# A tenth pair of chunks shares its weights in an attention and MoE kernel: the first chunk's transposed weights serve the fifth

## The chip, the cores and the metric

The kernel runs on one core of one Trainium2 chip. The metric is device time in microseconds (us): the median of three runs for the kernel before, and a profiled execution beside them that all rows below come from.

## What is computed

Two stages, cut from the reference to what matters here (8 batches, 2496 tokens, model width 256, key width 64, 8 experts of width 1024):

```python
scores = (1.0 / S) * np.matmul(z, z.transpose(0, 2, 1))
attn = np.maximum(scores, 0.0) ** 2
out = u * np.matmul(attn, v)
# then, on the rows of out with x @ w_skip > 0: top-1 expert, x + gate * (relu(x @ w1[e]) @ w2[e])
```

The scores of one batch are z times its own transpose, so the matrix of weights is symmetric: the weights of keys in group j for queries in chunk c are the transpose of those of keys in group c for queries in chunk j. The kernel uses this.

## The kernel before, in words

**Chunks and steps.** The queries of each batch are cut into five chunks of 512 tokens (the fifth has 448). I call them first to fifth; the code has c = 0 to 4. A chunk works through ten steps p = 0 to 9, each of 256 keys, so that steps 2j and 2j+1 are the keys of chunk j. `ORDER[c]` is the table that sets in which order a chunk takes its steps; batch 0's first chunk takes them 0 to 9. I call the position in that order the *place*, 0 to 9.

**One step.** `weights` (L322 to L338) makes the weights of a step: either it computes scores on TensorE (`scores`, L276, three pairs of half-row matmuls into `ps`) and ScalarE makes relu and square of them (L324, L325) in a tile `r`; or it takes `r` from memory (`recall`, L309 for a full chunk, L311 and L312 for the fifth). Then the high part `ah` is cast (L334, on ScalarE or VectorE as `on_act` says: on ScalarE for every step that belongs to a pair or stands in `EXTRA[c]`), and VectorE makes the low part `al` (L338). `attend` (L365) multiplies both with the values: up to 24 half-row matmuls for the two halves d = 0 and 1 of the width, and 18 for step 9, whose last keys are half a block.

**Pairs.** `PAIRS` lists the pairs (c, j) of chunks that share weights. For a pair, chunk c computes the steps of group j and `keep` (L293) turns them on VectorE, two transposes a step, into a tile `rt`; there are two such tiles for the whole kernel, and one pair fills one. When both steps are in, four stores (L720, 256 KB each) put the tile in a memory tensor `kept`. Chunk j later loads the two steps with `recall` and computes no scores for them. Batch 0 uses no pair with the first chunk.

**The order of the work.** The program is written out by hand, engine by engine, and each queue runs in order; SyncE (SP) issues the loads and stores. At each place the loop issues a recall five places ahead (`ahead`), makes weights two places ahead (`stage`), attends d = 0 of the step at hand and then d = 1. Place 8 attends only d = 0; place 9 ends the chunk, and its d = 1 work covers both. `keep` of the step at place 8 is put off by a place. What ends a chunk runs in the next one: row transposes of the output (L402) after places 1 and 2, stores `xr` and `out` (L411, four each) after places 3 and 4, and the stores of `kept` by `put_some` two places after their tile was filled. In every other first chunk (batches 1, 3, 5, 7) the routing of two chunks' tokens also runs, a run of small VectorE operations (L514 to L530 among them).

```python
t = turned_r[ci] = gp.tile([P, QC // 32, P], F32, name="rt", tag="rt", bufs=2)   # in keep, for even p
r = ap.tile([P, 2, QC], F32, name="r", tag="r", bufs=5)                          # in r_tile
after = [(rows0, 2), (rows1, 3), (store, 4), (store, 5)]                         # places after a chunk's end
```

Before the first load lands, TensorE runs `NWARM` small matmuls (L177). After the 40 chunks come the expert layers (L632, L651), which the change does not touch.

Of the kernel before, what the change touches and what calls it, by code (L numbers as in the profile page):

```python
# [22 lines left out]
NSTAT = 8  # L23
NFIX = 3
NARM = 2 * (NSTAT - NFIX)
NWARM = 35

PAIRS = ((0, 1), (0, 2), (0, 3), (1, 2), (1, 3), (1, 4), (2, 3), (2, 4), (3, 4))  # L30
ORDER = (
# [5 lines left out]
)  # L37
EXTRA = ((8,), (3,), (4, 5), (6, 7), (0, 1, 8))

# [9 lines left out]
def attn_moe(ctx, tc, zT, uT, v, wg, w1, w2, cst, pad, out):  # L49
# [125 lines left out]
    psw = ps_s.tile([P, 2, QC], F32, name="psw", tag="s")  # L175
    for _ in range(NWARM):
        nc.tensor.matmul(psw[:32, 0, :64], ones[:, :32], ones[:, :64], start=True, stop=True)  # L177
# [49 lines left out]
    def pairs(b):  # L227

        return PAIRS if b else [x for x in PAIRS if x[0]]

# [10 lines left out]

    kept = {x: dram.tile([QC, QC], F32, name="kept%d%d" % x) for x in PAIRS}
    HALF = (slice(0, 64), slice(64, 128))
# [804 lines left out]
```

## Time and profile before

| | us |
|---|---|
| median of three runs (lowest, highest) | 1758.07 (1756.36, 1759.94) |
| the profiled execution | 1756.26 |
| its span, first to last instruction | 1754.5 |
| TensorE busy (PE) | 1741.5 (99%) |
| VectorE busy (DVE) | 1176.2 (67%) |
| ScalarE busy (ACT) | 1154.4 (66%) |
| GpSimd busy (POOL) | 511.8 (29%) |
| DMA, mean over the span | 160 GB/s |

The attention part fills the first 1262 us or so of the span, the expert layers the rest. A chunk takes 27 to 35 us. In the rows, PE is TensorE, DVE VectorE, ACT ScalarE, SP SyncE; SPq is the issue of a transfer by SP. "out<-in" are tile names, and "[0.51 <-PE ps L276]" is idle time of the engine before the row and what ended it. Start times count from the start of the span.

### The profile page before, as it was taken

What the parts mean: (1) busy time and instruction counts of PE and PEld (TensorE: products, weight loads), DVE (VectorE), ACT (ScalarE), POOL (GpSimd) and SP (SyncE); (2) the same over time, 40 slices, a digit from 0 to 9 for tenths busy, and PEclk for the clock granted to TensorE, in tenths of its full rate; (3) what the DMA queues carried; (4) which work ended last, traced back from release to release, by engine and by line L of the source; (5) the groups of instructions that cost most, each with busy time, mean ns of one, the idle gap of its engine ahead of it and who ended that gap; (6) DMA issues with size and microseconds to landing.
All of it is one profiled execution on the core that took longest, in us unless ns stands there. A gap on an engine that the chain in (4) does not pass through costs nothing.

```text
span 1754.5 us, 39820 instructions
## 1 busy us (share of the span) xinstructions
PE 1741.5 (99%) x15783; PEld 1554.9 (89%) x15783; DVE 1176.2 (67%) x1912; ACT 1154.4 (66%) x1435; POOL 511.8 (29%) x516
## 2 busy tenths in 40 slices
PE   9999999999999999999999999999999999999998
PEld 7888888988888898888889888888999999999998
DVE  6877877787787788778778877777753433343333
ACT  8877877887787778778787887877533333333321
POOL 1102202212311221231222032122356456635731
PEclk9999999999999999999999999999999999999999
DMA  5667689387768848875784888477553323313210
GB/s 193 151 173 178 165 219 263 90 224 227 195 146 214 227 129 205 255 206 126 214 231 125 201 243 230 113 207 207 160 133 89 80 80 112 95 51 93 88 39 27
DMA packets 432353, 281.00 MB, mean 160 GB/s; under 512 B 213844, under 2 KB 370902, under 8 KB 432033
## 3 DMA queue, kind: packets, MB, share of 16 engines
q1 hardware_dynamic: 417888, 254.09, 54.3%
q0 software_dynamic: 13712, 22.99, 4.6%
q8 instruction: 138, 2.26, 0.5%
q14 instruction: 183, 1.49, 0.3%
q10 hardware_dynamic: 432, 0.17, 0.0%
HBM read 151.04 MB, written 126.78 MB: 158 GB/s over the span
## 4 chain that ended last, share of the span: by engine, by line
PE 92%; DMA 3%; issue 2%; DVE 1%; ACT 1%; POOL 1%; SPq 0%; POOLq 0%; DVEq 0%; ACTq 0%
PE acc L365 58%; PE psh L632 12%; PE y L651 11%; PE ps L276 10%; DMA out<-o,idt 2%; PE psm L433 1%; PE pst L600 1%; DVE al L338 1%; ACT ah L334 1%; DMA r<-kept 0%; DMA raw<-in_v 0%; POOL xgu L582 0%; DMA kept<-rt 0%; POOL out L681 0%; DMA xgu<-xr,go 0%
## 5 line engine op out<-in xcount | busy, mean ns | idle before, releaser
L365 PE MATMUL acc<-ah,vh 64*128 64x512 f32 (+1 forms) x3120 | 642.0, 384 | 0.8 <-ACT ah L334 0.4
L365 PE MATMUL acc<-ah,vl 64*128 64x512 f32 (+1 forms) x3120 | 627.6, 382 | 0.0
L338 DVE TENSOR_TENSOR al<-r,ah 128x1024 fp32r<-128x1024 f32 (+1 forms) x400 | 477.9, 1201 | 195.3 <-ACT ah L334 190.0
L365 PE MATMUL acc<-al,vh 64*128 64x512 f32 (+1 forms) x3120 | 496.2, 383 | 0.7 <-DVE al L338 0.2
L532 POOL DMA_INDIRECT lst<-pair,dest x160 | 195.6, 1222 | 771.2 <-DVE dest L530 739.8
L334 ACT CAST ah<-r 128x1024 fp32r<-128x1024 f32 (+1 forms) x349 | 355.3, 1029 | 43.7 <-PE acc L365 31.8
L324 ACT ACTIVATE r<-ps 128x1024 f32<-128x1024 f32 (+1 forms) x262 | 265.6, 1014 | 172.7 <-PE ps L276 164.0
L365 PEld LDWEIGHTS acc<-ah,vh 64*128 64x128 f32 x3120 | 329.2, 184 | 52.8 <-ACT ah L334 3.8
L365 PEld LDWEIGHTS acc<-ah,vl 64*128 64x128 f32 x3120 | 329.4, 184 | 44.3 <-DVE vl L121 0.3
L365 PEld LDWEIGHTS acc<-al,vh 64*128 64x128 f32 x3120 | 310.9, 184 | 52.1 <-DVE al L338 7.2
L637 ACT ACTIVATE hh<-psh 128x512 fp32r<-128x512 f32 (+1 forms) x172 | 98.9, 584 | 287.6 <-PE psh L632 245.6
L325 ACT ACTIVATE r<-r 128x1024 f32<-128x1024 f32 (+1 forms) x262 | 274.8, 1049 | 8.3
L632 PE MATMUL psh<-xt,w1h 128*128 128x256 f32 (+1 forms) x1280 | 235.7, 285 | 0.8 <-DVE o L680 0.8
L651 PE MATMUL y<-w2t,hh 128*128 128x256 f32 x1328 | 235.4, 280 | 0.0
L638 DVE SCALAR_TENSOR_TENSOR hl<-psh,hh 128x512 fp32r<-128x512 f32 (+1 forms) x172 | 113.2, 671 | 136.8 <-ACT hh L637 128.6
L651 PEld LDWEIGHTS y<-w2t,hh 128*128 128x128 f32 x1328 | 201.8, 188 | 0.0
L632 PEld LDWEIGHTS psh<-xt,w1h 128*128 128x128 f32 x1280 | 197.6, 189 | 1.7 <-DVE o L680 1.1
L651 PE MATMUL y<-w2t,hl 128*128 128x256 f32 x664 | 184.5, 278 | 0.9 <-DVE hl L638 0.9
L632 PE MATMUL psh<-xt,w1l 128*128 128x256 f32 (+1 forms) x640 | 182.1, 285 | 0.1
L293 DVE STREAM_TRANSPOSE rt<-r 128x512 f32<-128x512 f32 x276 | 179.1, 687 | 0.8 <-DMA kept<-rt 0.6
L651 PEld LDWEIGHTS y<-w2t,hl 128*128 128x128 f32 x664 | 124.7, 188 | 1.2 <-DVE hl L638 1.1
L681 POOL DMA_INDIRECT out<-o,idt x77 | 76.8, 998 | 166.5 <-DVE o L680 143.6
(182 smaller groups left out, 1642.7 us busy)
## 6 DMA issues: line engine op xcount, KB each, us to landing
kept<-rt SPq DMA_DIRECT2D x276, 256.0 KB, 5.0
r<-kept SPq DMA_DIRECT2D x90, 512.0 KB, 6.6
raw<-in_v SPq DMA_DIRECT2D x80, 256.0 KB, 5.9
r<-kept SPq DMA_DIRECT2D x48, 352.0 KB, 5.9
ut<-in_uT SPq DMA_DIRECT2D x32, 512.0 KB, 4.7
xr<-xrow SPq DMA_DIRECT2D x128, 128.0 KB, 3.1
out<-xrow SPq DMA_DIRECT2D x128, 128.0 KB, 2.9
raw<-in_w SPq DMA_DIRECT2D x64, 256.0 KB, 3.5
```

The source lines that it names most:

```text
L276: nc.tensor.matmul(to, k[h, o : o + P], queries(ci, q, h, n), start=(m == 0), stop=(m == 2))
L293: nc.vector.transpose(t[:, :, 32 * k : 32 * k + 32].rearrange("p (k a) i -> p a k i", k=4), r[:, x, :].rearrange("p (a k i) -> p a k i", a ...
L324: nc.scalar.activation(r[:, :, :n], ps[:, :, :n], AF.Relu, scale=isc)
L325: nc.scalar.activation(r[:, :, :n], r[:, :, :n], AF.Square)
L334: (nc.scalar.copy if on_act(ci, p) else nc.vector.tensor_copy)(h_, r_)
L338: nc.vector.tensor_sub(l_, r_, f32(h_))
L365: nc.tensor.matmul(acc[t][:, :n], w[h, x, dd], a[h, x, :n], start=(first and t not in halves[:m]), stop=(last and t not in halves[m + 1 :]),)
L532: put = nc.gpsimd.indirect_dma_start(out=lst, out_offset=bass.IndirectOffsetOnAxis(ap=dest[:, t : t + 1], axis=0), in_=pair[:, t, :], in_o ...
L632: nc.tensor.matmul(ps[:, j * W : (j + 1) * W], wt[:, a, o : o + P], x[:, d, :W], start=(m == 0), stop=(m == 5),)
L637: nc.scalar.activation(hh[:, : G * W], ps[:, : G * W], AF.Relu)
L638: nc.vector.scalar_tensor_tensor(hl[:, : G * W], ps[:, : G * W], 0.0, f32(hh[:, : G * W]), op0=ALU.max, op1=ALU.subtract)
L651: nc.tensor.matmul(ys[t], h[:, tt], w2t[f][:, k, :], start=(f == 0 and m == 0 and t % share == 0), stop=(f == NF - 1 and m == 2), skip_gro ...
```

## The change

A tenth pair (0, 4) is added: the first chunk computes and keeps the steps 8 and 9 for the fifth, which recalls steps 0 and 1 in place of computing them. The first chunk then takes step 0, the steps 2 to 9 that all belong to a pair, and step 1; the fifth takes step 8, the eight recalled ones and step 9. Two of the small matmuls at the start go.

```diff
-NWARM = 35
+NWARM = 33
...
-PAIRS = ((0, 1), (0, 2), (0, 3), (1, 2), (1, 3), (1, 4), (2, 3), (2, 4), (3, 4))
+PAIRS = ((0, 1), (0, 2), (0, 3), (0, 4), (1, 2), (1, 3), (1, 4), (2, 3), (2, 4), (3, 4))
 ORDER = (
-    (0, 1, 2, 3, 8, 4, 5, 6, 7, 9),
+    (0, 2, 3, 4, 5, 6, 7, 8, 9, 1),
...
-    (0, 2, 1, 3, 4, 5, 8, 6, 7, 9),
+    (8, 0, 1, 2, 3, 4, 5, 6, 7, 9),
 )
```

How this moves instructions, at the three places that the prediction speaks of.

TensorE at the start of the fifth chunk of batch 4 (its first rows of 448 columns), before:

```order
3084 L276 MATMUL ps<-zqh,zh 128x448 x2
3085 L276 MATMUL ps<-zql,zh 128x448 x2
3086 L276 MATMUL ps<-zqh,zl 128x448 x2
3087 L365 MATMUL acc<-ah,vh 128x448 x2
3088 L365 MATMUL acc<-ah,vl 128x448 x2
```

and with the change:

```order
3064 L365 MATMUL acc<-ah,vl 128x512 x2
3065 L365 MATMUL acc<-al,vh 128x512 x4
3066 L365 MATMUL acc<-ah,vh 128x448 x2
3067 L365 MATMUL acc<-ah,vl 128x448 x2
3068 L365 MATMUL acc<-ah,vh 128x448 x2
```

The three rows of scores (six matmuls) for step 1 are gone; a second such group goes in the same chunk.

SP from batch 3's fifth chunk (row 254, the `out` stores of the fourth) into batch 4's first chunk (from row 256 on), before (`kept_173` is the tensor of the first pair of that chunk):

```order
254 L411 DMA out<-xrow 32x16x64 x4
255 L167 DMA ut<-in_uT 128x2x512
256 L411 DMA xr<-xrow 32x14x64 x4
257 L720 DMA kept_173<-rt 32x16x128 x4
258 L411 DMA out<-xrow 32x14x64 x4
259 L167 DMA ut<-in_uT 128x2x512
```

and with the change (`kept_171` and `kept_172` are the tensors of that chunk's first and second pair):

```order
269 L411 DMA out<-xrow 32x16x64 x4
270 L167 DMA ut<-in_uT 128x2x512
271 L720 DMA kept_171<-rt 32x16x128 x4
272 L411 DMA xr<-xrow 32x14x64 x4
273 L411 DMA out<-xrow 32x14x64 x4
274 L720 DMA kept_172<-rt 32x16x128 x4
275 L167 DMA ut<-in_uT 128x2x512
```

The first pair's stores have moved ahead of `xr`, and the second pair's stores now stand behind all eight stores of `xr` and `out`.

VectorE in the first chunk of batch 4, from the low part of the step at place 4 on (with the semaphores that an instruction waits for; DMAHW are those of transfers), before:

```order
728 L338 TENSOR_TENSOR al<-r,ah 128x1024 [waits PE_49,Activation_49]
729 L402 STREAM_TRANSPOSE xrow<-ut 128x14x32
730 L338 TENSOR_TENSOR al<-r,ah 128x1024 [waits PE_49,Activation_49]
731 L293 STREAM_TRANSPOSE rt<-r 128x4x4x32 x2
732 L338 TENSOR_TENSOR al<-r,ah 128x1024 [waits PE_49,Activation_49]
733 L293 STREAM_TRANSPOSE rt<-r 128x4x4x32 x2
734 L338 TENSOR_TENSOR al<-r,ah 128x1024 [waits PE_49,Activation_49]
735 L293 STREAM_TRANSPOSE rt<-r 128x4x4x32 [waits DMAHW6_49,DMAHW7_49,DMAHW5_49,DMAHW4_49]
736 L293 STREAM_TRANSPOSE rt<-r 128x4x4x32
737 L338 TENSOR_TENSOR al<-r,ah 128x1024 [waits PE_49,Activation_49]
```

and with the change:

```order
731 L338 TENSOR_TENSOR al<-r,ah 128x1024 [waits PE_49,Activation_49]
732 L293 STREAM_TRANSPOSE rt<-r 128x4x4x32 x2
733 L402 STREAM_TRANSPOSE xrow<-ut 128x14x32
734 L338 TENSOR_TENSOR al<-r,ah 128x1024 [waits PE_49,Activation_49]
735 L293 STREAM_TRANSPOSE rt<-r 128x4x4x32 [waits DMAHW2_49,DMAHW1_49,DMAHW3_49,DMAHW0_49,DVE_49]
736 L293 STREAM_TRANSPOSE rt<-r 128x4x4x32
737 L338 TENSOR_TENSOR al<-r,ah 128x1024 [waits PE_49,Activation_49]
738 L293 STREAM_TRANSPOSE rt<-r 128x4x4x32 x2
739 L338 TENSOR_TENSOR al<-r,ah 128x1024 [waits PE_49,Activation_49]
740 L293 STREAM_TRANSPOSE rt<-r 128x4x4x32 [waits DMAHW6_49,DMAHW5_49,DMAHW7_49,DMAHW4_49,DVE_49]
741 L293 STREAM_TRANSPOSE rt<-r 128x4x4x32
742 L338 TENSOR_TENSOR al<-r,ah 128x1024 [waits PE_49,Activation_49]
```

Two transposes for the step at place 4 have come in ahead of the output's row transpose (row 733). The transposes at place 7 waited for the four stores of the chunk's first pair; now they wait for those of its second.

## Rows read from the trace of the kernel before

**Rows 1.** The page's busy times, with the share of the span.

```profile
PE 1741.5 (99%) x15783; PEld 1554.9 (89%) x15783; DVE 1176.2 (67%) x1912; ACT 1154.4 (66%) x1435; POOL 511.8 (29%) x516
```

**Rows 2.** The page's chain of waits, by line.

```profile
PE acc L365 58%; PE psh L632 12%; PE y L651 11%; PE ps L276 10%; DMA out<-o,idt 2%; PE psm L433 1%; PE pst L600 1%; DVE al L338 1%; ACT ah L334 1%; DMA r<-kept 0%; DMA raw<-in_v 0%; POOL xgu L582 0%; DMA kept<-rt 0%; POOL out L681 0%; DMA xgu<-xr,go 0%
```

**Rows 3.** Windows: length, busy us of PE, PEld, DVE, ACT, POOL; clock, DMA share, GB/s.

```profile
639.15:672.48 33.33, 33.33 (x297) 33.33 (x295) 24.63 (x32) 29.25 (x30) 7.83 (x8) 1.00 0.54 133
...
758.00:785.00 27.00, 27.00 (x262) 24.15 (x260) 21.21 (x34) 21.03 (x26) 12.07 (x10) 1.00 0.96 252
788.00:803.00 15.00, 15.00 (x162) 12.73 (x160) 12.42 (x16) 11.91 (x14) 0.00 (x0) 1.00 0.00 1
```

**Rows 4.** Timeline of PE, one group of scores in batch 4's fifth chunk.

```profile
777.22 0.37 PE L276 MATMUL ps<-zqh,zh 64*128 64x448 f32 x2
...
777.84 0.36 PE L365 MATMUL acc<-ah,vh 64*128 64x448 f32 x2
```

**Rows 5.** Timeline of PE, the first scores after the small matmuls.

```profile
4.55 0.80 PE L276 MATMUL ps<-zh 64*128 64x512 f32 x2 [1.50 <-ACT zh L109]
```

**Rows 6.** Groups by line and shape: the transposes of `keep`, busy us, mean ns.

```profile
L293 DVE STREAM_TRANSPOSE rt<-r 128x512 f32<-128x512 f32 x276 | 179.1, 687 | 0.8 <-DMA kept<-rt 0.6
```

**Rows 7.** Timeline of DVE, batch 4's first chunk.

```profile
650.66 0.64 DVE L402 STREAM_TRANSPOSE xrow<-ut 128x448 f32<-128x448 f32 x1
...
661.03 1.30 DVE L293 STREAM_TRANSPOSE rt<-r 128x512 f32<-128x512 f32 x2
...
665.43 0.69 DVE L334 CAST ah<-r 128x1024 fp32r<-128x1024 f32 x1 [1.09 <-ACT r L325]
666.23 1.23 DVE L338 TENSOR_TENSOR al<-r,ah 128x1024 fp32r<-128x1024 f32 x1
```

**Rows 8.** Timeline of DVE, batch 5's first chunk.

```profile
807.09 0.64 DVE L402 STREAM_TRANSPOSE xrow<-ut 128x448 f32<-128x448 f32 x1
...
817.74 1.30 DVE L293 STREAM_TRANSPOSE rt<-r 128x512 f32<-128x512 f32 x2
818.96 0.18 DVE L514 TENSOR_REDUCE sm<-ex 128x8 f32<-128x64 f32 x1
...
820.68 1.23 DVE L338 TENSOR_TENSOR al<-r,ah 128x1024 fp32r<-128x1024 f32 x1
822.06 0.69 DVE L334 CAST ah<-r 128x1024 fp32r<-128x1024 f32 x1 [0.16 <-ACT r L325]
```

**Rows 9.** Timeline of SP: batch 4's first chunk, then batch 7's second.

```profile
651.33 2.00 SPq L411 DMA_DIRECT2D xr<-xrow  x4
653.37 3.90 SPq L720 DMA_DIRECT2D kept<-rt  x4
...
1153.88 2.84 SPq L411 DMA_DIRECT2D xr<-xrow  x4
1156.77 2.44 SPq L411 DMA_DIRECT2D out<-xrow  x4
1159.31 3.79 SPq L720 DMA_DIRECT2D kept<-rt  x4
```

**Rows 10.** Line L720 from 653.2 to 657.0: first and last issue, landing.

```profile
L720 SPq DMA_DIRECT2D kept<-rt x4: 546/971/1282, 653.4 to 656.0; - x4
...
DMA to landing us min/median/max: 3.6/4.9/5.0
```

**Rows 11.** Timeline of PE: place 8 of batch 4's first chunk, of batch 5's.

```profile
666.36 0.50 PE L365 MATMUL acc<-ah,vh 64*128 64x512 f32 x2
...
823.10 0.39 PE L365 MATMUL acc<-ah,vh 64*128 64x512 f32 x2
```

**Rows 12.** Timeline of ACT, batch 4's first chunk, relu of place 4.

```profile
646.28 1.03 ACT L324 ACTIVATE r<-ps 128x1024 f32<-128x1024 f32 x1 [0.51 <-PE ps L276]
```

**Rows 13.** Timeline of DVE, the low part at place 2 of that chunk.

```profile
770.62 1.09 DVE L338 TENSOR_TENSOR al<-r,ah 128x896 fp32r<-128x896 f32 x1 [0.74 <-ACT ah L334]
```

**Rows 14.** Line L311 (recalls of the fifth chunks), us from issue to landing.

```profile
DMA to landing us min/median/max: 4.9/5.9/7.5
```

## The prediction

> **What bounds the kernel now.** I read the busy times first: TensorE is busy for 99% of the span, VectorE and ScalarE for two thirds [rows 1]. Busy is not yet bound, so I read the chain of waits by line next: 58% of it is `attend`, 10% the scores, and VectorE and ScalarE lines have 1% each [rows 2]. The windows say the same of single stretches: in batch 4's first chunk TensorE is busy for 33.33 of 33.33 us, VectorE for 24.63 and ScalarE for 29.25 [rows 3]. What leaves TensorE therefore shows in the time, and what comes to another engine is free as long as its result still arrives before TensorE wants it. The question of this change is whether it does.
>
> **What the change removes.** In each of seven batches two groups of scores of the fifth chunk go, 14 groups in all. A group is three pairs of matmuls; from its first row to the first row behind it are 777.84 - 777.22 = 0.62 us [rows 4]. 14 x 0.62 = 8.7 us, all on the path that sets the end. Their 28 relu and square go from ScalarE, which costs nothing there and saves nothing, since ScalarE doesn't end last. Batch 0 only takes its fifth chunk in another order, with as many scores: nothing, within one such group's 0.62 us either way.
>
> **What costs nothing.** Two small matmuls: TensorE waits 1.50 us for ScalarE's first cast before its first scores, whatever ends before [rows 5]; the clock in the windows is 1.00 [rows 3] and I let it stand. Four transposes more in each first chunk, 0.69 us each [rows 6], are 2.7 us of VectorE, less one cast (0.69, rows 7) that goes to ScalarE: 24.63 + 2.1 of 33.33 us. ScalarE gets one cast more there on 29.25 us, about as long as its other passes over a step (1.03, rows 12). Both fit as sums [rows 3]. The first pair's stores now issue between 788 and 803, by batch 4's clock, where the DMA share is 0.00 [rows 3]. If these covers were gone, each would cost its own length, seven times.
>
> **What is late next.** The first chunk now fills four `rt` tiles in places 1 to 8, two places each, where before it filled three with a gap. There are two tiles, so the transposes at place 7 wait until the *second* pair's stores have landed, and these stand in SP's queue behind eight stores of `xr` and `out`, which wait for the row transposes L402, which now stand behind the transposes of place 4. Behind the waiting transposes, on VectorE, are the low part of place 8, the cast and the low part of place 9: TensorE wants all three. I work out this wait.
>
> *When `xr` starts.* The second row transpose starts at 650.66 and takes 0.64, and `xr` is issued at 651.33 [rows 7, 9]. Two transposes come in ahead (817.74 to 818.96, 1.22 us, rows 8), and ScalarE's extra cast of about 1.0 us meets 0.51 of idle time ahead of place 4 and some more ahead of place 2 [rows 12]; I let it push the low part back by 0.3, between ends of 0 and 0.5: 650.66 + 1.22 + 0.3 + 0.64 = 652.8. In the odd batches 807.09 + 1.22 + 0.64 = 809.0 (VectorE had idle time there, so the 0.3 is not added).
>
> *From there to the landing.* Four `xr` stores of this size take 653.37 - 651.33 = 2.04 us of SP; four `out` stores straight behind `xr` took 1159.31 - 1156.77 = 2.54; four `kept` stores from first issue to last landing 656.0 + 4.9 - 653.37 = 7.6 us [rows 9, 10]. Together 12.2, and 0.1 for the wait to end. From below: `out` as quick as `xr`, and the shortest landing of the row behind the last issue, 2.04 + 2.04 + 2.6 + 3.6 = 10.3. From above: `xr` 2.89 as in the second chunk, 13.0. I take 12.2, as two of its terms come from this very place. The tiles are free at 652.8 + 12.3 = 665.1 in batch 4, at 809.0 + 12.3 = 821.3 in batch 5; VectorE would have turned at 661.03 and 817.74 [rows 7, 8].
>
> *What TensorE feels.* Step 9, now at place 8, has 9 matmuls for d = 0, or 4.5 pairs of 0.227 (0.68 / 3 of a full group), 1.02 us; place 8 starts at 666.36 and 823.10 [rows 11]. So TensorE wants the low part of place 9 at 666.36 + 1.02 + 0.91 = 668.29 and 825.03. VectorE delivers it in batch 4 at 665.1 + 1.22 (transposes) + 1.12 (low part of place 8) + 0.80 (cast, 665.43 to 666.23) + 1.23 = 669.5: 1.2 us late [rows 7]. In batch 5 the small routing operations stand in between, 820.68 - 818.96 = 1.72 us, and the step to the cast is 1.22: 821.3 + 1.22 + 1.72 + 1.22 + 0.80 + 1.23 = 827.5, 2.5 us late [rows 8]. Three even batches (2, 4, 6) and four odd ones (1, 3, 5, 7): 3 x 1.2 + 4 x 2.5 = 13.6 us.  By the lower bound of the landing it is 0 and 0.6, some 2.4 in all; by the upper one 2.0 and 3.3, some 19.
>
> That the wait exists can be seen before: there VectorE lost 0.6 us in all to stores of `kept` [rows 6], with the first pair's stores, issued 4 us earlier against the same transposes, landing at 661.0 for transposes at 661.03.
>
> **The sum.** -8.7 + 13.6 = +4.9 us on the profiled execution's 1756.3, 1761.2. The median of the runs shown is 1.8 above that execution, so 1763.0 for the median. With the bounds of the landing: -6.3 to +10.3, or 1751.8 to 1768.4.
>
> **Rivals.**
>
> *Hidden after all (faster).* The second pair's stores land soon enough: where they are free by 663.8 and 818.8, nothing is late. For it: VectorE has 24.63 us of work in 33.33 [rows 3], the routing could slip into idle time, and the mechanism leaves 0.6 us in all now [rows 6]. Against it: both `xr` and `out` have to pass SP first, 4.1 us at the quickest. It gives -8.7: 1749.4. The point from which it decides is a landing within 9.8 us of `xr`'s first issue, which is where the odd batches lose nothing; at 11 us there remain 3.5 us of gain. This is the case that a page of the Trainium skill would have: "DMA: Bandwidth & Descriptors", in "Anatomy of one DMA", gives a transfer 2.0 us and its bytes at 436 GB/s, which makes 2.6 us of a 256 KB store, an estimate from the page. The stores would then land 2.3 us sooner than I have them, the wait would cost under 1 us in all, and the sum would be about -8. The row has 4.9 us for such a store with others in flight [rows 10], so the trace speaks against the page here, and I don't raise the chance for it.
>
> *Recalls late (slower still).* In 758 to 785, around the start of the fifth chunk, the DMA share is 0.96 at 252 GB/s [rows 3]; two more recalls of 0.46 MB there (128 x 2 x 448 floats) are 0.92 / 252 = 3.6 us of such transfers. Besides, with five `r` tiles the recall for place 5 takes the tile of place 2, now a recalled step, so that it can't be issued before that step's low part is made. In its old place at 770.62 this low part waited for a cast [rows 13]; the cast comes sooner now, the work in front of it on VectorE stays, and I take 770.8 for its end. It lands 5.9 us later at the median, 7.5 at the longest [rows 14]: 776.7 to 778.3; cast and low part take some 2.1, so 778.8 to 780.4. Place 4 starts at 777.22 without its scores [rows 4], and place 5 12 pairs of 0.207 later, at 779.7; the low part is wanted 0.8 behind. So it fits, by about 1.7 us at the median, and just so at the longest. Each us beyond the longest would cost 7 us: with one, 1763.0 + 7 = 1770.0.
>
> **How the numbers follow.** Forecast, the wait on the `rt` tiles eats the gain and some more, 0.66; hidden 0.20; recalls late on top of it 0.14. The forecast's own range is 1751.8 to 1768.4. The range reaches down to the hidden case and leaves most of the late recalls out: 1749.4 to 1768.4. A measurement of this kernel tells about 0.2% from no change, 3.5 us. Of the forecast's 0.66 I give 0.03 to faster, 0.26 to within 0.2% and 0.37 to slower; of the hidden case 0.18 to faster and 0.02 to within; of the late recalls 0.02 to within and 0.12 to slower. Together faster 0.21, same 0.30, slower 0.49.
>
> **What would show it.** The fifth chunks of batches 1 to 7 shorter by 1.2 us, with no gaps of TensorE in them. In the first chunks the transposes L293 at place 7 waiting some 4 us for `kept`, in sum about 27 us over seven batches where it was 0.6; TensorE's gaps at places 8 and 9, in front of `al` and `ah`, larger in odd batches than in even ones. If that wait is under 15 us in all, or the chunks' lengths don't grow, the forecast's step from VectorE to TensorE is wrong; if ScalarE or TensorE waits for recalls in the fifth chunk, the third case holds.

## The result, and the profile after

| | before | after |
|---|---|---|
| median, us (lowest, highest), six runs each | 1757.93 (1756.36, 1759.94) | 1766.47 (1765.00, 1769.65) |
| the profiled execution, us | 1756.26 | 1765.72 |
| its span, us | 1754.5 | 1763.9 |

The ratio is 1.0050 with an interval of 1.0037 to 1.0063: the change made the kernel slower by half a per cent. 1763.0 was forecast, slower, with 1749.4 to 1768.4 as the range.

The busy times of the page after (against [rows 1]):

```profile
PE 1742.3 (99%) x15697; PEld 1543.7 (88%) x15697; DVE 1186.7 (67%) x1933; ACT 1134.8 (64%) x1414; POOL 511.2 (29%) x516
```

TensorE has 86 records fewer and yet the same busy time; a busy TensorE is, as the page warns, not one at its peak. So I measure what matters chunk by chunk. The start of a chunk is the start of its first matmul of `attend` (L365) in the trace; the table has the time from one to the next, in us, before and after, summed over batches 1 to 7.

| | first chunks | second | third | fourth | fifth |
|---|---|---|---|---|---|
| growth, batches 1 to 7 | +12.5 | +1.3 | +0.1 | -4.3 | -3.1 |
| one even batch (4), before to after | 33.33 to 34.00 | 32.41 to 32.52 | 30.88 to 30.90 | 31.73 to 31.11 | 26.98 to 26.42 |
| one odd batch (5), before to after | 34.74 to 36.73 | 30.83 to 31.06 | 32.22 to 32.30 | 30.29 to 29.69 | 28.42 to 27.74 |

These five sums are +6.5. Batch 0 with its start adds 1.7, and what follows the attention (its end went from 1262.44 to 1270.60) another 1.3: together the 9.5 between the two profiled executions. The gain is there, 0.6 in every fourth chunk and 0.45 to 0.7 in the fifth ones but for batch 6's, which grew by 0.4: 7.4 in all. The first chunks take it back and two thirds as much again.

Where it goes, the waits over the whole span say. First those before, then those after: engine and line, what was waited for, us in total, times, longest.

```profile
PEld acc L365 <- DVE al L338: 7.2, 18, 0.6
ACT ah L334 <- DMA r<-kept: 5.1, 7, 1.3
DVE rt L293 <- DMA kept<-rt: 0.6, 2, 0.4
```

```profile
DVE rt L293 <- DMA kept<-rt: 28.5, 9, 4.2
ACT ah L334 <- DMA r<-kept: 27.9, 26, 2.8
PEld acc L365 <- DVE al L338: 18.9, 30, 2.3
PE acc L365 <- DVE al L338: 6.1, 6, 1.9
```

VectorE's transposes wait 28.5 us for stores of `kept` (0.6 before), and TensorE now waits for `al`. ScalarE's wait for recalls has grown as well, by 22.8 us, but little of it reaches TensorE, whose weight loads wait 3.8 us for ScalarE's casts of `ah` in both profiles; I come back to the part that does.

The windows of batch 4's and batch 5's first chunk (columns as in [rows 3], where batch 4's had 33.33 of 33.33 us):

```profile
644.80:678.80 34.00, 33.86 (x296) 30.00 (x294) 26.40 (x35) 29.97 (x31) 7.12 (x8) 1.00 0.67 163
799.76:836.49 36.73, 35.55 (x332) 28.69 (x329) 30.60 (x56) 30.21 (x33) 5.52 (x4) 1.00 0.63 158
```

VectorE has 26.40 us of work in 34.00: it isn't full. TensorE is idle all the same, by 1.18 us in batch 5; in batch 4 only by 0.14, since the ends of matmuls are modelled and cover most of a short stall, and there the lost time shows in the chunk's length. The chain in batch 4, SP's queue first, then VectorE's (against [rows 7, 9]):

```profile
651.85 3.45 SPq L720 DMA_DIRECT2D kept<-rt  x4
658.30 1.93 SPq L411 DMA_DIRECT2D xr<-xrow  x4
660.28 2.48 SPq L411 DMA_DIRECT2D out<-xrow  x4
662.80 3.63 SPq L720 DMA_DIRECT2D kept<-rt  x4
```

```profile
661.74 1.30 DVE L293 STREAM_TRANSPOSE rt<-r 128x512 f32<-128x512 f32 x2 [1.86 <-DMA kept<-rt]
...
665.44 1.23 DVE L338 TENSOR_TENSOR al<-r,ah 128x1024 fp32r<-128x1024 f32 x1
670.19 1.30 DVE L293 STREAM_TRANSPOSE rt<-r 128x512 f32<-128x512 f32 x2 [3.53 <-DMA kept<-rt]
671.42 1.18 DVE L338 TENSOR_TENSOR al<-r,ah 128x1024 fp32r<-128x1024 f32 x1
672.52 0.68 DVE L334 CAST ah<-r 128x1024 fp32r<-128x1024 f32 x1
673.31 1.22 DVE L338 TENSOR_TENSOR al<-r,ah 128x1024 fp32r<-128x1024 f32 x1
```

The second pair's stores are issued from 662.80, behind all eight of `xr` and `out`; the tile is free for the transposes at 670.19, 11.9 us after `xr`'s first issue; and the low part of place 9 starts at 673.31 behind it. The first row, at place 5, is a wait of another kind, for the *first* pair's stores; only batches 4 and 6 have it, and VectorE has made it good before place 7. In batch 5 the run of routing operations lies between the transposes (826.13) and the low parts of place 8 (829.06) and place 9 (831.00), and TensorE stands still longer. It stops at place 8 already (VectorE's row, then PE's, which wants this low part):

```profile
829.06 1.23 DVE L338 TENSOR_TENSOR al<-r,ah 128x1024 fp32r<-128x1024 f32 x1
```

```profile
830.34 0.73 PE L365 MATMUL acc<-al,vh 64*128 64x512 f32 x3 [1.03 <-DVE al L338]
```

### The profile page after: what moved, and what is told of

Same layout as the page of the kernel before. It is cut to its first block, busy times and chain, and to the rows that moved or that the text cites. A ratio compares the mean times of both kernels' runs of the same rounds, so it can differ in the third digit from the quotient of the medians.

```text
span 1763.9 us, 39749 instructions
## 1 busy us (share of the span) xinstructions
PE 1742.3 (99%) x15697; PEld 1543.7 (88%) x15697; DVE 1186.7 (67%) x1933; ACT 1134.8 (64%) x1414; POOL 511.2 (29%) x516
## 4 chain that ended last, share of the span: by engine, by line
PE 79%; DMA 7%; ACT 4%; DVE 4%; SPq 3%; issue 3%; POOL 0%; POOLq 0%; DVEq 0%; ACTq 0%
PE acc L365 48%; PE psh L632 11%; PE y L651 11%; PE ps L276 7%; DMA kept<-rt 2%; DMA out<-o,idt 2%; SPq L411 2%; ACT ah L334 2%; DMA r<-kept 2%; DVE al L338 1%; ACT r L325 1%; PE psm L433 1%; ACT r L324 1%; DVE rt L293 1%; PE pst L600 1%
## 5 line engine op out<-in xcount | busy, mean ns | idle before, releaser
L365 PE MATMUL acc<-ah,vh 64*128 64x512 f32 (+1 forms) x3120 | 653.5, 385 | 1.0 <-ACT ah L334 0.4
L365 PE MATMUL acc<-ah,vl 64*128 64x512 f32 (+1 forms) x3120 | 639.1, 383 | 0.0
L365 PE MATMUL acc<-al,vh 64*128 64x512 f32 (+1 forms) x3120 | 509.5, 384 | 7.3 <-DVE al L338 6.1
L334 ACT CAST ah<-r 128x1024 fp32r<-128x1024 f32 (+1 forms) x356 | 362.7, 1029 | 79.2 <-PE acc L365 39.3
L365 PEld LDWEIGHTS acc<-ah,vh 64*128 64x128 f32 x3120 | 342.4, 185 | 56.5 <-ACT ah L334 3.8
L365 PEld LDWEIGHTS acc<-ah,vl 64*128 64x128 f32 x3120 | 343.3, 185 | 45.5 <-DVE vl L121 0.3
L365 PEld LDWEIGHTS acc<-al,vh 64*128 64x128 f32 x3120 | 316.8, 184 | 64.7 <-DVE al L338 18.9
L324 ACT ACTIVATE r<-ps 128x1024 f32<-128x1024 f32 (+1 forms) x248 | 252.6, 1019 | 146.6 <-PE ps L276 127.3
L325 ACT ACTIVATE r<-r 128x1024 f32<-128x1024 f32 (+1 forms) x248 | 261.4, 1054 | 7.9
L293 DVE STREAM_TRANSPOSE rt<-r 128x512 f32<-128x512 f32 x304 | 197.3, 687 | 28.5 <-DMA kept<-rt 28.5
```

What stands on the lines that cost most here:

```text
L293: nc.vector.transpose(t[:, :, 32 * k : 32 * k + 32].rearrange("p (k a) i -> p a k i", k=4), r[:, x, :].rearrange("p (a k i) -> p a k i", a ...
L324: nc.scalar.activation(r[:, :, :n], ps[:, :, :n], AF.Relu, scale=isc)
L325: nc.scalar.activation(r[:, :, :n], r[:, :, :n], AF.Square)
L334: (nc.scalar.copy if on_act(ci, p) else nc.vector.tensor_copy)(h_, r_)
L365: nc.tensor.matmul(acc[t][:, :n], w[h, x, dd], a[h, x, :n], start=(first and t not in halves[:m]), stop=(last and t not in halves[m + 1 :]),)
```

## The experiments

All kernels ran beside the kernel before, in three series: in the first it took 1769.1 us, in the other two 1757.4 and 1757.8. What differs is what follows the attention, above all the expert layers: it takes 503 to 507 us in the traces of the first series and 492 to 495 in the others, for a reason that isn't known; so I compare inside a series only. Chunk times are read as above.

**The second pair's stores ahead of `out`.** Edit on the changed kernel, at the head of a place's later work (in a first chunk, place 4 is where `out` is issued):

```diff
+        if ci % NQ == 0 and k == 4:
+            put_some()
         for f in todo.pop(s, []):
```

> The changed kernel, but in the first chunk the second pair's four stores are issued between xr and out instead of behind both. Theory 1 (the transposes at place 7 wait for these stores): they land about 2.0 + 7.6 = 9.6 us behind the first xr instead of 11.9, so the even batches lose nothing and the odd ones at most 0.2 us; of the 12.5 us that the first chunks of batches 1 to 7 grew by, some 12 go, and the kernel comes out 2 to 6 us below the kernel before. The waits of VectorE for stores of kept fall from 28.5 us to about 12 in all and TensorE shows none of them. Rival (the first chunk has too much work for VectorE and ScalarE, whatever the stores do): stays 7 to 10 us above the kernel before.

Measured: 0.9989 (0.9977 to 1.0001), and once more in the third series:

> The change with the second pair's stores ahead of `out` by hand, once more, beside the other cure of the same wait: if the earlier ratio of 0.999 was held up by the low-clock stretches of that series' expert layers and by late recalls, 0.997 to 0.999; if moving the stores by hand is worth as much as the new order, the same as with the order, 0.998.

There 0.9989 (0.9980 to 0.9998). The waits of VectorE for stores and of TensorE for `al`, in the first of the two:

```profile
DVE rt L293 <- DMA kept<-rt: 11.1, 8, 1.6
PEld acc L365 <- DVE al L338: 9.4, 20, 0.7
```

And the windows of its first chunks of batches 4 and 5:

```profile
637.30:670.62 33.32, 33.32 (x298) 30.56 (x295) 26.86 (x35) 29.99 (x31) 8.11 (x8) 1.00 0.65 156
791.51:826.53 35.02, 35.02 (x331) 29.92 (x329) 30.61 (x56) 30.23 (x33) 5.51 (x4) 1.00 0.64 151
```

SP issues the four stores from 653.23 on, between `xr` and `out`. With nothing else moved, the first chunks are back at 33.32 and 35.02 (before 33.33 and 34.74), TensorE busy throughout, though VectorE makes every one of the added transposes. Of the first chunks' 12.5 us, 0.4 are left, 0.9 in the repeat: the place of four stores in SP's queue is nearly the whole cost. The gain that this should set free, 8 us and more, does not come in full: only 1 to 2 us faster than before, and the first of the two intervals includes no change at all. The largest part of what is missing is in the fifth chunk of batch 6, 30.83 us where batch 4 has 26.42 (28.80 in the repeat); in the first of the two the granted clock stood at 0.50 for 3.4 us in that chunk, and batch 2's fifth is long as well, 27.73. Another 1.3 and 0.6 are in the second chunks.

**The order alone**, with the nine pairs of before:

```diff
-PAIRS = ((0, 1), (0, 2), (0, 3), (0, 4), (1, 2), (1, 3), (1, 4), (2, 3), (2, 4), (3, 4))
+PAIRS = ((0, 1), (0, 2), (0, 3), (1, 2), (1, 3), (1, 4), (2, 3), (2, 4), (3, 4))
```

> The changed kernel without the pair (0, 4): the new orders of the first and fifth chunk and the 33 small matmuls alone. Theory 1: the third pair's transposes now stand at places 5 and 6 and wait for the first pair's stores, which land in time; no more than 2 us of waits for kept, and the time within 3 us of the kernel before. Rival (the new order itself, with seven or eight steps in a row on ScalarE, is what costs): 5 us or more above the kernel before, with TensorE waiting for ScalarE's casts in the first chunks.

Measured: 1.0020 (1.0010 to 1.0030). The first chunks keep 33.3 and 34.8, so the order without the fourth tile costs nothing there. Fourth chunks grow by 0.6 and fifth shrink by 0.3: with nine pairs, three computed steps stand in a row across that border (8, 0, 1). In the changed kernel only batch 0 has these three, and there the fourth chunk grew by 0.67 and the fifth shrank by 0.31. So the new orders cost something by themselves where the tenth pair is missing, but not in the first chunks.

**The two small matmuls back:**

```diff
-NWARM = 33
+NWARM = 35
```

> The changed kernel with 35 small matmuls again. Theory A (the start is the same but for chance): within 1.5 us of the changed kernel, that is 7 to 10 us above the kernel before. Rival B (two matmuls fewer let TensorE's clock rise later, which the profile of the changed kernel shows at 15.4 us against 13.2): the first chunk of batch 0 ends about 1.3 us earlier again, the kernel 6 to 8 us above the kernel before.

Measured: 1.0053 (1.0037 to 1.0069), as the change itself. They decide nothing. This run is of use for something else, below: the granted clock fell in two of its first chunks and in batch 6's fifth.

**The kernel before, with its first pair's stores behind `xr` and `out`:**

```diff
-            if puts and puts[0][0] < step[0] - 1:
+            if puts and puts[0][0] < step[0] - 1 - (step[0] // NP % NQ == 0 and step[0] % NP == 3):
```

> The kernel before, with nothing added but this: in the first chunk the first pair's four stores are issued behind xr and out instead of between them, so that the transposes at place 7 find their tile as late as in the changed kernel. Theory 1, by the prediction's own sum: the stores land 2.04 + 2.54 + 7.6 = 12.2 us behind xr, at 663.5 in batch 4 and 820.0 in batch 5; VectorE is late by nothing in even batches (the low part of place 9 at 668.0, wanted at 668.4) and by 1.1 us in odd ones: 4 us above the kernel before, with 10 to 20 us of waits of VectorE for kept. Rival (VectorE has enough slack, the wait is not what TensorE feels): within 1.5 us of the kernel before, in spite of these waits.

The added term holds these stores back while the first chunk is at place 3. Measured: 1.0028 (1.0016 to 1.0039), VectorE's wait for `kept` 16.6 us, odd first chunks longer by 0.6 to 1.2, even ones by 0 to 0.45. So the same wait can be put into the kernel before, with no pair added, and it costs there too.

**The pairs one place earlier.** A third `rt` tile, which should take the wait away directly, is not tested here. Tested is an order of the first chunk that fills the first two tiles sooner:

```diff
-    (0, 2, 3, 4, 5, 6, 7, 8, 9, 1),
+    (2, 3, 4, 5, 0, 6, 7, 8, 1, 9),
```

> The change with the first chunk's steps in the order 2 to 5, 0, 6, 7, 8, 1, 9 and no store moved by hand: the first and the second pair are complete one place sooner, and in SP's queue the second pair's stores then stand between `xr` and `out`. If the wait on these stores is what costs, first chunks of batches 1 to 7 come back to 33.3 (even) and 34.8 (odd), the transposes wait for `kept` under 15 us in all, and the ratio is about 0.999, as with the stores moved by hand. If it is the four more transposes on VectorE that cost, the chunks stay at 34.0 and 36.7 or more, and the ratio at 1.005.

> The change with the first chunk's order 2 to 5, 0, 6, 7, 8, 1, 9, once more, beside the two others: 0.998 again.

Measured: 0.9980 (0.9971 to 0.9989) in the second series, 0.9987 (0.9978 to 0.9996) in the third. SP's queue in batch 4 of the first of them, and VectorE's waits:

```profile
650.30 2.01 SPq L411 DMA_DIRECT2D xr<-xrow  x4
652.36 3.80 SPq L720 DMA_DIRECT2D kept<-rt  x4
656.20 3.73 SPq L411 DMA_DIRECT2D out<-xrow  x4
```

```profile
DVE rt L293 <- DMA kept<-rt: 6.5, 7, 1.8
```

The stores stand between `xr` and `out` by the order alone, and the wait is down to 6.5 us. Even first chunks are at 33.4, odd ones at 35.2, 0.47 over before, with a gap of 0.5 us in front of a group of scores. This order also moves the last pair's second step to place 9, so by itself it would prove less than the edit by hand; but the two edits have only the stores' place in common, and they cure the same chunks.

**The change again**, beside these:

> The change as it is, beside the others on this chip: ratio 1.004 to 1.006 if its loss doesn't depend on the chip.

Measured: 1.0059 (1.0046 to 1.0073), with the waits of the first profile (27.9 us for `kept`) and first chunks longer by 12.4 us.

**The ninth step earlier in the fifth chunk**, first with the stores moved by hand, then with the new first order:

```diff
-    (8, 0, 1, 2, 3, 4, 5, 6, 7, 9),
+    (8, 0, 1, 2, 9, 3, 4, 5, 6, 7),
```

> The change with the second pair's stores ahead of `out`, and in the fifth chunk the computed step 9 at place 4 instead of 9, so that steps 3 to 7, all recalled, come one place (2.6 us) later. If the rest of the loss there is recalls that land late (gaps of 0.6 to 1.5 us at places 8 and 9 of batches 2 and 6), these gaps go: fifth chunks of 26.4 (even) and 27.7 (odd) in every batch, attention 7 to 8 us shorter than before, ratio about 0.996. If the transfers have too little room there whatever the order, the fifth chunks stay uneven (one of 30, one of 27.7) and the ratio stays at about 0.999.

> The change with both new orders (first chunk 2 to 5, 0, 6, 7, 8, 1, 9; fifth chunk 8, 0 to 2, 9, 3 to 7), no store moved by hand. If both waits, on stores in the first chunk and on recalls in the fifth, are what ate the gain, it returns: first chunks 33.3 and 34.8, fifth chunks 26.4 and 27.7, ratio about 0.996. If only the first, about 0.999; if neither, 1.005.

Measured: 1.0016 (1.0006 to 1.0025) and 1.0015 (1.0006 to 1.0024), both worse than without the edit. Neither expectation had foreseen what happened: the last fifth chunk takes 33 us instead of 27. Its rows in the first of the two, TensorE's weight loads and then its matmuls:

```profile
1238.04 0.18 PEld L276 LDWEIGHTS ps<-zqh,zh 64*128 64x128 f32 x2 [2.26 <-DVE cnt_e L550]
```

```profile
1257.50 0.47 PE L365 MATMUL acc<-ah,vh 64*128 64x448 f32 x2 [2.54 <-ACT ah L334]
```

The scores of step 9 now come just when a count of the routing holds their PSUM tile, which only batch 7 has there, and a late recall comes after it; behind that wait the granted clock is 0.50 for 3.4 us. In batches 2, 4 and 6 the fifth chunks take 26.4 to 27.5 in the first kernel and 27.8 to 28.4 in the second, so the edit doesn't settle whether the recalls have too little room.

**The loads among the recalls two places later**, on the kernel with the pairs earlier:

```diff
-                later(s0 + c * NB + 2 * k - 7, 7, load, b + 1, j, nc.vector)
+                lead = 5 if c == NQ - 1 else 7
+                later(s0 + c * NB + 2 * k - lead, lead, load, b + 1, j, nc.vector)
```

> The change with the first chunk's order 2 to 5, 0, 6, 7, 8, 1, 9, and the next batch's loads of v and z, which stand among the recalls of the fifth chunk, issued two places (5.3 us) later. If the transfers are what makes recalls late there (in batch 6 the DMA queues moved 8.17 MB in the 34 us around the fifth chunk, 240 GB/s, and two recalls came 1.3 and 0.7 us late), the late recalls get rarer: fifth chunks of 26.4 and 27.7 in all batches, 2 to 3 us less than with the order alone, ratio about 0.9965. If it is the slow stretches themselves (90 to 140 GB/s for some us), whatever is queued, nothing changes: 0.998.

Measured: 0.9977 (0.9968 to 0.9985); the interval overlaps that of the same kernel without the edit in this series (0.9987), and batch 6's fifth chunk still takes 28.05 us. Not enough to call it a gain. What makes that chunk long is seen in windows of the kernel without the edit, in the third series:

```profile
1083.00:1087.00 4.00, 4.00 (x40) 3.46 (x38) 2.74 (x3) 2.92 (x4) 3.69 (x4) 1.00 1.14 267
1087.00:1091.00 4.00, 4.00 (x40) 3.54 (x38) 3.44 (x5) 1.46 (x2) 0.10 (x1) 1.00 0.58 101
1091.00:1095.00 4.00, 3.87 (x36) 2.97 (x36) 1.72 (x2) 1.84 (x3) 1.62 (x2) 1.00 1.10 307
1095.00:1103.71 8.71, 8.02 (x74) 6.62 (x72) 7.04 (x10) 8.62 (x11) 0.87 (x1) 1.00 0.68 158
```

For four us the queues move 101 GB/s, between 267 and 307. The last recall was issued just ahead of this, and ScalarE waits for it; SP's row, then ScalarE's:

```profile
1085.31 0.38 SPq L311 DMA_DIRECT2D r<-kept  x1
```

```profile
1094.62 0.94 ACT L334 CAST ah<-r 128x896 fp32r<-128x896 f32 x1 [0.85 <-DMA r<-kept]
...
1095.98 0.91 ACT L324 ACTIVATE r<-ps 128x896 f32<-128x896 f32 x1
```

The recall took over 9 us with its second part (L312), the relu of step 9 stands behind its cast in ScalarE's order, and TensorE is idle for 0.7 us of the last window. The kernel before meets such a hole too, three us long around the start of the same chunk (1079.30), and TensorE doesn't feel it:

```profile
1077.50:1080.50 3.00, 3.00 (x30) 2.65 (x30) 2.83 (x4) 2.49 (x5) 0.46 (x1) 1.00 0.81 81
```

With eight recalled steps in the fifth chunk instead of six there is less slack for one, as I read it; that the extra recalls and not the moment of the hole decide is not shown.

The fastest kernels are those with the pairs earlier: 1753.3 and 1754.8 us against 1757.4 and 1757.8 of before, 0.13 to 0.2% faster, and in the second series 0.8% faster than the change as it was made (1768.0). With the loads later it is 1753.8 against 1757.8. All three intervals lie below 1; the gain of 0.13 to 0.23% is about as large as the 0.2% that the prediction takes for what a measurement can tell.

## Why the prediction was right, and where not

The direction and the mechanism came as forecast; the median is 3.5 us above the 1763.0, inside the range, and part of that closeness is luck, as the terms show.

**The gain** was forecast at 14 groups of 0.62, 8.7 us. Where nothing else disturbs them, batch 4's fourth and fifth chunks lost 0.62 and 0.56, batch 5's 0.60 and 0.68: the term stands. In sum the two columns have -7.4; the missing 1.3 are in fifth chunks, above all batch 6's, which grew by 0.4. The sign that was named, each fifth chunk shorter by 1.2 us, did not come: weights are made two places ahead, so one of the two groups used to stand before the fifth chunk's first `attend`, and its 0.6 us leave the fourth chunk.

**What is late next** was named rightly, down to the place. From `xr` to the free tile 12.3 us were forecast and 11.9 came, term by term (`xr` 1.98, `out` 2.52, the stores to the free tile 7.39, against 2.04, 2.54 and 7.7); in the chunk's own time the transposes were expected at 665.1 - 639.15 = 25.95 and came at 670.19 - 644.80 = 25.39; in batch 5 at 26.82 forecast, 826.13 - 799.76 = 26.37 measured. The wait at place 7 was put at about 27 us in all and is 25.3; the rest of the 28.5 are the two waits at place 5, 1.86 and 1.37 us in batches 4 and 6, which the forecast didn't have. The two cures and the same wait in the kernel before show that it is this, and not VectorE's added work.

**What TensorE feels** was mis-sized both ways. The sum, 3 x 1.2 + 4 x 2.5 = 13.6, came to 12.5: 2.1 in the three even ones and 10.4 in the four odd ones. By kind: even batches lost 0.7 each, as the transposes were 0.6 sooner than forecast; the odd ones 2.0 in batches 5 and 7, where they were 0.45 sooner, 2.5 in batch 1, where they came 0.5 later than in batch 5, and 3.9 in batch 3. That 10.4 stands so near the forecast 10.0 is luck: two odd batches fell short, and batch 3 made up for them. Its transposes started at 512.60, 27.24 us into the chunk, 0.9 later than in batch 5. The other 1.1 us, an estimate from these differences, go with a lower clock: the step "the clock in the windows is 1.00 and I let it stand" failed here. These are VectorE's row, the row of TensorE behind the stall, and windows around the stall, after it, and behind that:

```profile
512.60 1.31 DVE L293 STREAM_TRANSPOSE rt<-r 128x512 f32<-128x512 f32 x2 [4.16 <-DMA kept<-rt]
```

```profile
516.81 0.90 PE L365 MATMUL acc<-al,vh 64*128 64x512 f32 x3 [1.90 <-DVE al L338]
```

```profile
513.40:516.80 3.40, 1.51 (x14) 0.93 (x10) 3.19 (x11) 2.08 (x2) 0.90 (x1) 1.00 1.01 312
517.30:520.50 3.20, 3.20 (x17) 2.50 (x16) 3.10 (x6) 0.12 (x1) 2.20 (x3) 0.50 0.97 268
521.00:524.00 3.00, 3.00 (x28) 2.49 (x28) 1.56 (x2) 2.30 (x3) 1.42 (x2) 1.00 0.75 185
```

The granted clock is 0.50, that is 1.2 GHz, with 17 matmul records in 3.20 us where 28 fit into the 3.00 that follow.

**What I had at nothing.** The second chunks grew by 1.3 in all; with the stores moved by hand it is 1.3 and 0.6, with the pairs earlier nearly gone, and how it comes about isn't settled. Batch 0's other order was put at nothing within 0.62, and its fourth and fifth chunks together grew by 0.36. Its start and first chunk were 1.3 later in this profile; in the second profile of the same program they were 1.0 earlier than before. That is a difference between executions, not of the change. What follows the attention took 1.3 us more here, 2.5 in the second profile, and 0.2 to 2.4 in the other kernels of the last two series; this stays open.

So the forecast's +4.9 against the profile's +9.5 is made up of -1.1 in the first chunks, +1.3 in the second, +1.3 of gain that did not arrive, 1.7 in batch 0 and 1.3 at the end, which are 4.5 of the 4.6 us; 0.1 is in the third chunks.

**The rivals.** "Hidden after all" has fallen: its deciding point was a landing within 9.8 us of `xr`'s first issue, and the tile was free after 11.9. The page that the prediction names for this rival, the Trainium skill, "DMA: Bandwidth & Descriptors", has its 2.0 us and 436 GB/s in the section "Anatomy of one DMA — SWDGE (gpsimd) path", for transfers that GpSimd issues; from it comes the estimate of 2.6 us for 256 KB. The stores of `kept` are issued by SP, four at a time with others in flight, which that section does not cover; so the trace shows that the estimate doesn't carry over to them, not that it is wrong where it was made. The median of all such stores after is 5.0 us:

```profile
kept<-rt SPq DMA_DIRECT2D x304, 256.0 KB, 5.0
```

"Recalls late" is partly true, but not as priced. I had looked at place 5, where the recall is issued latest, and at 7 us per us, in every batch alike. (The low part of [rows 13] on which this rests is one of batch 4's fifth chunk, not of its first.) That place held. What came late was the last recall, for place 8, and behind it place 9, a computed step whose relu stands behind that recall's cast in ScalarE's order. It is batch 6 above all, whose fifth chunk is longer by 1.0 us in the first profile, 2.6 in the second and 1.6 to 4.4 in the cured kernels that keep the change's order there (against batch 4's 26.42; the stretch at the clock of 0.50 is part of the 4.4); in batch 2, where it came at all, by up to 1.3.

```profile
1108.15 0.47 PE L365 MATMUL acc<-ah,vh 64*128 64x448 f32 x2 [0.19 <-DVE ah L334]
1109.35 0.67 PE L365 MATMUL acc<-al,vh 64*128 64x448 f32 x3 [0.31 <-DVE al L338]
```

These are place 9 of batch 6 in the first profile. Median durations to landing, on which that step went, say nothing of a single hole in the transfers.

## What to carry to other kernels

When work is added to a ring of few buffers, look for the transfer that frees the buffer and for what stands ahead of it in its queue: here four stores behind eight others cost more than 14 groups of matmuls gave, and moving them, or filling the buffer one step sooner, took nearly all of that cost away, with the same matmuls. A saving on the bounding engine that is paid with transfers has to be checked against the worst stretch of the transfers, not against their median. And sum the change chunk by chunk, since TensorE's busy time was the same to 0.8 us where the kernel lost 9.5.

## What was not expected of the hardware

TensorE's granted clock fell to half for over 3 us in the midst of a program that keeps it busy for 99% of the span, after it had waited once for 1.90 us (batch 3, above). Not after each such wait: batch 1 of the same profile has 1.59 us of idle time in the same place with the clock at 1.00 after it, and with 35 small matmuls the same stall of batch 1, 1.57 us, was followed by this:

```profile
204.20:207.20 3.00, 3.00 (x16) 2.29 (x16) 2.90 (x6) 0.90 (x2) 2.10 (x2) 0.50 0.81 262
```

In the first kernel with the stores moved by hand it fell behind a wait of only 1.18 us, in batch 6's fifth chunk. What decides is open. And the transfers have holes of some us in which their rate falls to a third with work queued (101 GB/s above); batch 6's fifth chunk lost time in every kernel with ten pairs. Whether the holes go with the time or with the place in the program no run here tells.
